# New order of steps in the late and the early pairs of an attention-and-MLP kernel, and weights put together 1024 columns at a time

## The chip, the cores and the metric

The kernel runs on one core of a Trainium2 chip. The metric is the device time of one execution in microseconds (us). Engines are named as in the profile: PE (matrix products), PEld (its weight loads), DVE (vector engine), ACT (scalar engine), POOL (GpSimd), SP (the queue that issues the DMA transfers).

## The reference

Block-causal attention over 8 batches, 8 heads, 576 positions and 64 dimensions, and then a gated MLP on the 4608 rows of 512 that come out:

```
scores = scale * q @ k.T                    # masked by blocks of 64
attn   = exp(scores - max) / (sum + 1e-9)
x      = attn @ v                           # -> (4608, 512)
a = x @ w1 ; b = x @ w2                     # (512, 1024) each
out = ((a * b) @ w3) @ w_out                # (1024, 1024), (1024, 512)
```

The four weights are 64-bit floats; q, k and v are 32-bit.

## The kernel before, in words

The work is cut into 32 *pairs* (8 batches times 4 pairs of heads; one head is half j = 0 of the pair, the other j = 1). For each half the scores are computed in five tiles in PSUM, exponentiated by ACT, and multiplied with V. In the late pairs each 32-bit operand is split into a high and a low part, so that three products of a faster format give 32-bit accuracy.

**Early pairs 0 to 3** run while the weights arrive. `gen_w` loads the weights as pairs of 32-bit words, and `load_w` (L135) makes 32-bit floats of them on ACT (L150) and DVE (L151, L152, L155). `load_split` (L159) and `load_rows` (L164) then split w1 and w2 into high and low parts. The product w3 @ w_out is formed on PE (L388) and split (L376, L377). One call of the generator handles 512 columns of 128 rows, 512 KB of DMA.

**Late pairs 4 to 31** mix attention with the MLP: `gen_moe` works on blocks of 512 rows. For each of 8 blocks *f* of the hidden size it runs 8 steps of three matmuls (L412), then DVE multiplies both sides (L418), ACT makes the high part (L419) and POOL the low part (L420). Then come 4 x 8 steps of the second product (L430). After the last pair, the rest of the MLP runs alone.

The order of a pair is a string of letters, one for each half: `PLAN` (L44) for the late pairs, `EARLY_PLAN` (L49) for the early ones. The letters:

- S: one of the five score tiles (L243), then ACT's exponentials (L258, L259), DVE's subtract for the low part (L261) and POOL's running row sum (L264)
- V: one of five steps of the product with V (L306, early L282); V5 is the last and reads the 64-column low part that L261 wrote last
- F: one step of three matmuls of the MLP
- M: one step of `shift_mask` for the next pair: first ACT's casts (L171), then six groups of matmuls (L192) each followed by DVE's row maxima (L196); at the eighth step L198, a transpose on PE (*mt*, L200), ACT's negation (L202) and a DMA (L209) that writes the shift into qk
- A, B: `prep_qk` for the next pair's half 0 and for the pair's own half 1: a cast (L171, DVE), then a DMA that copies the high part (L219) and a subtract (L220, POOL in the late pairs); B also sends the other half of the shift and, at its second step, starts the load of the next pair's q and k (L100)
- R: DVE's sum over the row sums (*part*, L319); N: takes the result out of PSUM (L337, L338); T: a matmul of the sums (*tot*, L323), the reciprocal, and the division (L325 to L350)
- Q: brings in V for the next pair; C: one call of `gen_w`

The score tiles and the mask groups have two PSUM buffers each, so every second one waits for its reader; *tot* and *mt* use the same two buffers as the mask groups.

In the late pairs PE runs exactly in the written order. All other engines, and PE in the early pairs, are ordered ahead of time by a planner that takes what is ready by its own estimates, with the written order as priority; the early attention has a higher priority than the weights. The first six F are left out (`DELAY`), so that each late pair begins at the third step of an f block.

Of the kernel before, what the change touches and what calls it, by code (L numbers as in the profile page):

```python
# [7 lines left out]
F32 = mybir.dt.float32  # L8
# [4 lines left out]
ALU = mybir.AluOpType  # L13
# [3 lines left out]
P = 128  # L17
B, H, S, D = 8, 8, 576, 64
# [4 lines left out]
DF = 1024  # L23
NT = B * S
NC = DM // P
NF = DF // P
# [5 lines left out]
BIG = 8.0e9  # L32

PC = [0, 576, 1024, 1344, 1536]
PW = 1600
QLO = [0, 128, 256, 384, 512]
# [1 line left out]
PE = [0, 448, 768, 960, 1024]  # L40

PLAN = (  # L44
    "B F B S S F F B S S F F F F S M F F V V F V V F F R V F Q N F",
    "M A S F S F A S M F M S F M S F M A M V V V F F V V N Q R T M F F F",
)

EARLY_PLAN = (  # L49
    "M S S S C S C C C C M S V V B C M M V A V M V M Q B M A B M N",  # L50
    "S C C S A S S C S C V V V V V Q N T",
)

DELAY = 6
# [5 lines left out]
def block_causal_attention__then__gated_mlp_kernel(ctx, tc, qkv, consts, ident_in, w1, w2, w3t, wout, out_t):  # L60
    nc = tc.nc
    w1, w2, w3t, wout = (w.bitcast(I32) for w in (w1, w2, w3t, wout))
# [13 lines left out]
    w1l = cpool.tile([P, NC, DF], F32R, name="w1l")  # L76
    wh = cpool.tile([P, NF, DM], F32R, name="wh")
    wl = cpool.tile([P, NF, DM], F32R, name="wl")

    qk = [cpool.tile([P, 4, S], F32R, name=f"qk{j}") for j in range(2)]
# [7 lines left out]
    tl = {}  # L91
# [40 lines left out]
        tl["gh"] = pool.tile([P, NF, TB], F32R, name="gh")  # L132
        tl["gl"] = pool.tile([P, NF, TB], F32R, name="gl")

    def load_w(dst, src, k):  # L135

        t = tl["early"].tile([P, 1024], F32, tag="wraw", name="wraw", bufs=5)
        u = tl["early"].tile([P, 512], F32, tag="wbits", name="wbits", bufs=6)
        wide = t.bitcast(I32)
        nc.sync.dma_start(out=wide.rearrange("p (k w) -> p k w", k=k), in_=src)
        wide = wide.rearrange("p (c two) -> p c two", two=2)
        low, high = wide[:, :, 0], wide[:, :, 1]
        bits = u.bitcast(I32)
        V = nc.vector
        nc.scalar.activation(u, high.bitcast(F32), AF.Abs, scale=2.0**-112)  # L150
        V.tensor_scalar(out=bits, in0=bits, scalar1=3, scalar2=0x7FFFFFF8, op0=ALU.logical_shift_left, op1=ALU.bitwise_and)  # L151
        V.scalar_tensor_tensor(out=bits, in0=high, scalar=-0x80000000, in1=bits, op0=ALU.bitwise_and, op1=ALU.bitwise_or)  # L152
        if dst is None:
            dst = u.unsqueeze(1)
        V.scalar_tensor_tensor(out=dst.bitcast(I32), in0=low.rearrange("p (k w) -> p k w", k=k), scalar=29,  # L155
                               in1=bits.rearrange("p (k w) -> p k w", k=k), op0=ALU.logical_shift_right, op1=ALU.bitwise_or)
        return u

    def load_split(dst_h, dst_l, src):  # L159
        val = load_w(None, src.unsqueeze(1), 1)  # L160
        nc.scalar.copy(dst_h, val)
        nc.vector.tensor_tensor(out=dst_l, in0=val, in1=dst_h, op=ALU.subtract)

    def load_rows(dst_h, dst_l, src, c):  # L164
        for h in range(2):
            cs = slice(h * 512, (h + 1) * 512)
            load_split(dst_h[:, c, cs], dst_l[:, c, cs], src[c * P : (c + 1) * P, h * 1024 : (h + 1) * 1024])
            yield

    def cast(n, dst, src, act):  # L170
        (nc.scalar.copy if 0 < n <= EARLY or act else nc.vector.tensor_copy)(dst, src)  # L171
# [193 lines left out]

    def gen_w(wp):
        wo = tl["wo"]
        for k in range(NF):
            load_w(wo[:, k : k + 1, :], wout[k * P : (k + 1) * P, :].unsqueeze(1), 1)
            yield  # L370
        rows1 = (None for c in range(NC) for _ in load_rows(w1h, w1l, w1, c))
        pending = []

        def evacuate():
            m, acc = pending.pop(0)
            nc.scalar.copy(wh[:, m, :], acc)  # L376
            nc.vector.tensor_tensor(out=wl[:, m, :], in0=acc, in1=wh[:, m, :], op=ALU.subtract)  # L377

        for m in range(NF):
            t3 = wp.tile([P, NF, P], F32, tag="w3", name="w3", bufs=2)  # L380
            for k in range(0, NF, 4):
                src = w3t[k * P : (k + 4) * P, 2 * m * P : 2 * (m + 1) * P].rearrange("(k p) f -> p k f", p=P)
                load_w(t3[:, k : k + 4, :], src, 4)
                if k == 0:
                    yield
            acc = ps_m.tile([P, 512], F32, tag="psm", name=f"w{m}")
            for k in range(NF):
                nc.tensor.matmul(acc, t3[:, k, :], wo[:, k, :], start=(k == 0), stop=(k == NF - 1))  # L388
            pending.append((m, acc))
            if len(pending) > 1:  # L390
                evacuate()
            yield
            next(rows1)
            yield
        while pending:
            evacuate()
        for c in range(NC):
            yield from load_rows(w2h, w2l, w2, c)

    def gen_moe(k):  # L400
        mp, xh, xl, gh, gl = tl["late"], tl["xh"], tl["xl"], tl["gh"], tl["gl"]
        sides = ((w1h, w1l), (w2h, w2l))
        for f in range(NF):
            fs = slice(f * P, (f + 1) * P)
            acc = [ps_m.tile([P, TB], F32, tag="psm", name="ab") for _ in sides]
            order = [(i, c) for i in range(2) for c in range(NC)]
            if f == 0:
                order.sort(key=lambda ic: (ic[1] == NC - 1, ic))
            for i, c in order:
                a, b2 = sides[i]  # L410
                for s, (l, r) in enumerate(((a, xh), (b2, xh), (a, xl))):
                    nc.tensor.matmul(acc[i], l[:, c, fs], r[c], start=(c == 0 and s == 0), stop=(c == NC - 1 and s == 2))  # L412
                if (i, c) == (0, NC - 1):
                    a32 = mp.tile([P, TB], F32, tag="a32", name="a32", bufs=2)
                    nc.scalar.copy(a32, acc[0])
                if (i, c) != order[-1]:
                    yield
            nc.vector.tensor_tensor(out=a32, in0=acc[1], in1=a32, op=ALU.mult)  # L418
            nc.scalar.copy(gh[:, f, :], a32)  # L419
            nc.gpsimd.tensor_tensor(out=gl[:, f, :], in0=a32, in1=gh[:, f, :], op=ALU.subtract)  # L420
            if f == NF - 1:
                st["free"] = k + 1
                split_ready()
            yield
        for e in range(DM // P):
            t = ps_m.tile([P, TB], F32, tag="psm", name="o")
            es = slice(e * P, (e + 1) * P)
            for f in range(NF):
                for s, (l, r) in enumerate(((wh, gh), (wl, gh), (wh, gl))):
                    nc.tensor.matmul(t, l[:, f, es], r[:, f, :], start=(f == 0 and s == 0), stop=(f == NF - 1 and s == 2))  # L430
                if f < NF - 1:
                    yield
            o32 = mp.tile([P, TB], F32, tag="o32", name="o32")
            nc.scalar.copy(o32, t)
            nc.sync.dma_start(out=out_t[es, k * TB : (k + 1) * TB], in_=o32)
            yield
# [16 lines left out]
    def pair(n):  # L453
# [9 lines left out]
        for j in range(2):  # L463
# [2 lines left out]
            tiles = iter(S_TILES)  # L466
            pvs = (pv_early if early else pv)(n, j, xps, p_early)
            delay = DELAY if n == NPAIR and j == 0 else 0
            for step in (EARLY_PLAN if early else PLAN)[j].split():
                if step == "C":  # L470
                    fill(weights, 1)
                    continue
# [101 lines left out]
```

## Time and profile before

| | |
|---|---|
| runs shown | 1099.05, 1101.97, 1103.21 us; median 1101.97 |
| profiled execution | 1099.04 us, span 1097.3 us |
| PE busy | 988.5 us (90%) |
| DVE busy | 777.6 us (71%) |
| ACT busy | 535.6 us (49%) |
| POOL busy | 527.3 us (48%) |
| mean granted clock of PE | 0.966 |
| moved by DMA | 80.12 MB |

Busy shares are means over stages with different limits, and a matmul's end is modelled, so a busy PE is not PE at its peak. What matters is which engine waits for which, stage by stage.

### The profile page before, as it was taken

What the parts mean: (1) busy time and instruction counts of PE and PEld (TensorE: products, weight loads), DVE (VectorE), ACT (ScalarE), POOL (GpSimd) and SP (SyncE); (2) the same over time, 40 slices, a digit from 0 to 9 for tenths busy, and PEclk for the clock granted to TensorE, in tenths of its full rate; (3) what the DMA queues carried; (4) which work ended last, traced back from release to release, by engine and by line L of the source; (5) the groups of instructions that cost most, each with busy time, mean ns of one, the idle gap of its engine ahead of it and who ended that gap; (6) DMA issues with size and microseconds to landing.
All of it is one profiled execution on the core that took longest, in us unless ns stands there. A gap on an engine that the chain in (4) does not pass through costs nothing.

```text
span 1097.3 us, 13914 instructions
## 1 busy us (share of the span) xinstructions
PE 988.5 (90%) x4608; PEld 763.6 (70%) x4608; DVE 777.6 (71%) x1284; ACT 535.6 (49%) x1265; POOL 527.3 (48%) x449
## 2 busy tenths in 40 slices
PE   4799978989988898899999898899889988999998
PEld 2454557777777777777777677677777777888887
DVE  7899987877888678877887777777877887611010
ACT  4565655555455554545555544545554455422121
POOL 0000075665567455755666555754675567423020
PEclk9899989999999999999999999999999999999999
DMA  7867311222222222222112222221222211000001
GB/s 242 257 222 247 90 49 52 56 75 75 56 57 62 68 65 56 56 63 75 36 54 64 75 56 56 65 85 45 56 56 84 66 45 33 30 10 10 29 1 39
DMA packets 37112, 80.12 MB, mean 73 GB/s; under 512 B 4464, under 2 KB 12784, under 8 KB 37040
## 3 DMA queue, kind: packets, MB, share of 16 engines
q1 hardware_dynamic: 37040, 79.23, 24.6%
q8 instruction: 36, 0.59, 0.2%
q14 instruction: 36, 0.29, 0.1%
HBM read 50.76 MB, written 9.44 MB: 55 GB/s over the span
## 4 chain that ended last, share of the span: by engine, by line
PE 60%; DVE 28%; ACT 6%; issue 5%; DMA 1%; SPq 0%; ACTq 0%; DVEq 0%
PE ab L412 28%; PE o L430 16%; DVE m L196 7%; DVE ph L261 6%; PE s L243 6%; DVE pl L261 5%; PE x L306 4%; PE w L388 3%; DVE qk L171 2%; ACT rsum L258 2%; DVE part L319 2%; ACT ph L259 1%; PE tot L323 1%; DVE qk L220 1%; DVE wbits L152 1%
## 5 line engine op out<-in xcount | busy, mean ns | idle before, releaser
L264 POOL TENSOR_TENSOR rsum<-rsum,p 128x448 f32<-128x448 f32 x224 | 184.4, 823 | 113.8 <-ACT p L258 86.7
L420 POOL TENSOR_TENSOR gl<-a,gh 128x512 fp32r<-128x512 f32 x72 | 98.1, 1362 | 196.4 <-ACT gh L419 196.4
L243 PE MATMUL s<-qk 128*128 128x288 f32 (+4 forms) x768 | 164.1, 320 | 17.4 <-ACT ph L259 5.3
L261 DVE TENSOR_TENSOR pl<-p,ph 128x448 fp32r<-128x448 f32 x168 | 152.6, 922 | 37.7 <-ACT ph L259 36.1
L243 PEld LDWEIGHTS s<-qk 128*128 128x128 f32 (+1 forms) x768 | 123.4, 185 | 51.0 <-ACT ph L259 10.9
L220 POOL TENSOR_TENSOR qk<-rqk,qk 64x1152 fp32r<-64x1152 f32 x54 | 148.4, 2748 | 18.3 <-DVE qk L171 18.2
L233 POOL TENSOR_TENSOR vs<-rv,vs 128x320 fp32r<-128x320 f32 x56 | 49.2, 880 | 189.6 <-ACT vs L171 189.6
L196 DVE TENSOR_REDUCE m<-mx 128x1 f32<-128x512 f32 (+6 forms) x320 | 129.8, 446 | 5.0 <-PE mx L192 3.6
L259 ACT ACTIVATE ph<-s 128x288 fp32r<-128x288 f32 x336 | 131.4, 392 | 0.0
L412 PE MATMUL ab<-xh,w1h 128*128 128x512 f32 x288 | 126.1, 438 | 0.1
L418 DVE TENSOR_TENSOR a<-ab,a 128x512 f32<-128x512 f32 x72 | 49.2, 683 | 103.0 <-PE ab L412 102.3
L430 PE MATMUL o<-gh,wh 128*128 128x512 f32 x288 | 120.7, 419 | 0.0
L412 PE MATMUL ab<-xh,w2h 128*128 128x512 f32 x288 | 118.9, 413 | 0.0
L412 PE MATMUL ab<-xh,w1l 128*128 128x512 f32 x288 | 118.1, 410 | 0.0
L412 PE MATMUL ab<-xl,w1h 128*128 128x512 f32 x288 | 118.0, 410 | 0.0
L430 PE MATMUL o<-gh,wl 128*128 128x512 f32 x288 | 116.6, 405 | 0.0
L430 PE MATMUL o<-gl,wh 128*128 128x512 f32 x288 | 116.2, 403 | 0.0
L412 PE MATMUL ab<-xl,w2h 128*128 128x512 f32 x288 | 114.7, 398 | 0.0
L258 ACT ACTIVATE p<-s 128x448 f32<-128x448 f32 x224 | 86.1, 384 | 58.2 <-PE s L243 41.4
L412 PE MATMUL ab<-xh,w2l 128*128 128x512 f32 x288 | 114.1, 396 | 0.0
L306 PE MATMUL x<-ph,vs 128*128 128x128 f32 x336 | 89.7, 308 | 13.6 <-DVE ph L261 13.6
L192 PE MATMUL mx<-kb,qd 128*128 128x512 bf16 (+6 forms) x320 | 73.6, 297 | 25.4 <-DVE m L196 18.1
(69 smaller groups left out, 1796.6 us busy)
## 6 DMA issues: line engine op xcount, KB each, us to landing
qk<-qk SPq DMA_DIRECT2D x64, 288.0 KB
rqk<-in_qkv SPq DMA_DIRECT2D x31, 576.0 KB
rv<-in_qkv SPq DMA_DIRECT2D x32, 320.0 KB
out_t<-o SPq DMA_DIRECT2D x36, 256.0 KB
wraw<-in_w3t SPq DMA_DIRECT2D x16, 512.0 KB
wraw<-in_w SPq DMA_DIRECT2D x16, 512.0 KB
wraw<-in_wout SPq DMA_DIRECT2D x8, 512.0 KB
qk<-ms SPq DMA_DIRECT2D x64, 2.2 KB
```

What stands on the lines that cost most here:

```text
L192: nc.tensor.matmul(sc, qd[:, i, :], kb[:, a:b], start=True, stop=True)
L196: nc.vector.reduce_max(m[:, col : col + 1], sc, axis=AX.X)
L220: (nc.vector if n <= EARLY else nc.gpsimd).tensor_tensor(out=low, in0=rqk[o], in1=high, op=ALU.subtract)
L243: nc.tensor.matmul(t[ks, at : at + q1 - q0], qk[j][:, 2 + s, kr], qk[j][:, s, q0:q1], start=(s == 0), stop=(s == 1))
L258: nc.scalar.activation(p32, t[ks, at : at + w], AF.Exp, scale=SCALE)
L259: nc.scalar.activation(ph[ks, o : o + w], t[ks, at : at + w], AF.Exp, scale=SCALE)
L261: nc.vector.tensor_tensor(out=low, in0=p32, in1=ph[ks, o : o + w], op=ALU.subtract)
L264: nc.gpsimd.tensor_tensor(out=r, in0=r, in1=p32, op=ALU.add)
L306: nc.tensor.matmul(xps[:, to : to + w], v[:, c, :], parts[s][:, a : a + w], start=(u < 2 and s == 0), stop=((u, s) in ((0, 1), (len(PV) - ...
L412: nc.tensor.matmul(acc[i], l[:, c, fs], r[c], start=(c == 0 and s == 0), stop=(c == NC - 1 and s == 2))
L420: nc.gpsimd.tensor_tensor(out=gl[:, f, :], in0=a32, in1=gh[:, f, :], op=ALU.subtract)
L430: nc.tensor.matmul(t, l[:, f, es], r[:, f, :], start=(f == 0 and s == 0), stop=(f == NF - 1 and s == 2))
```

## The change

Three things are edited. The late pair's two strings are new; both orders hold 24 F, 10 S and 10 V. The early pairs get a pair of strings each instead of one common pair; C stands 20 times in all instead of 40. And `load_w` takes a width: w_out and w3 come in loads of 1024 columns (1 MB), as do the rows of w1 (one row block whole) and of w2 (two row blocks, half the columns each). The buffers of a load go from five of 1024 words to three of 2048, those of the bits from six of 512 to two of 1024. `load_split` is folded into `load_rows`. An assertion at build time was added, which issues nothing.

```diff
 PLAN = (
-    "B F B S S F F B S S F F F F S M F F V V F V V F F R V F Q N F",
-    "M A S F S F A S M F M S F M S F M A M V V V F F V V N Q R T M F F F",
+    "F F F F F S F S F B S F F B S F M F S F F V V V V V Q M R N F",
+    "S S M F S F F S M F V S M R M F F V F F V V M F V N Q F T A A M",
 )
 EARLY_PLAN = (
-    "M S S S C S C C C C M S V V B C M M V A V M V M Q B M A B M N",
-    "S C C S A S S C S C V V V V V Q N T",
+    ("S S S V S S C V C B M C M M A V V V M N M B M M Q M",
+     "S S C S A V C S S V V V V Q N T C"),
+    ("C M S S V S M C V C S V B C S A V V M M Q B M N A M",
+     "S M S M C S V V S V S V V N T Q"),
+    ("M B M S S S B V C S V S V V V Q N M",
+     "S S V M A S M V S A C M C S M V V M V N T Q"),
+    ("S C B C S V S C S S B V M V A M M V M V N Q",
+     "C S S M S S V V S V A V V Q C N M T M C M"),
 )
...
-    def load_w(dst, src, k):
-        t = tl["early"].tile([P, 1024], F32, tag="wraw", name="wraw", bufs=5)
-        u = tl["early"].tile([P, 512], F32, tag="wbits", name="wbits", bufs=6)
+    def load_w(dst, src, k, n=1024):
+        t = tl["early"].tile([P, 2 * n], F32, tag="wraw", name="wraw", bufs=3)
+        u = tl["early"].tile([P, n], F32, tag="wbits", name="wbits", bufs=2)
...
+    def load_rows(dst_h, dst_l, src, c, k, cs):
+        rows = src[c * P : (c + k) * P, 2 * cs.start : 2 * cs.stop].rearrange("(k p) f -> p k f", p=P)
+        val = load_w(None, rows, k, k * (cs.stop - cs.start))
+        nc.scalar.copy(dst_h[:, c : c + k, cs], val)
+        nc.vector.tensor_tensor(out=dst_l[:, c : c + k, cs], in0=val, in1=dst_h[:, c : c + k, cs], op=ALU.subtract)
...
-        for k in range(NF):
-            load_w(wo[:, k : k + 1, :], wout[k * P : (k + 1) * P, :].unsqueeze(1), 1)
+        for k in range(0, NF, 2):
+            load_w(wo[:, k : k + 2, :], wout[k * P : (k + 2) * P, :].rearrange("(k p) f -> p k f", p=P), 2)
             yield
...
-            for k in range(0, NF, 4):
-                src = w3t[k * P : (k + 4) * P, 2 * m * P : 2 * (m + 1) * P].rearrange("(k p) f -> p k f", p=P)
-                load_w(t3[:, k : k + 4, :], src, 4)
-                if k == 0:
-                    yield
+            load_w(t3, w3t[:, 2 * m * P : 2 * (m + 1) * P].rearrange("(k p) f -> p k f", p=P), NF)
...
-            next(rows1)
-            yield
+            if m % 2:
+                load_rows(w1h, w1l, w1, m // 2, 1, slice(0, DF))
+                yield
...
-        for c in range(NC):
-            yield from load_rows(w2h, w2l, w2, c)
+        for h in range(2):
+            for c in (0, 2):
+                load_rows(w2h, w2l, w2, c, 2, slice(h * 512, (h + 1) * 512))
+                yield
...
-            for step in (EARLY_PLAN if early else PLAN)[j].split():
+            for step in (EARLY_PLAN[n] if early else PLAN)[j].split():
```

More of the change, by code (lines that the diff above doesn't have):

```diff
@@ L44 @@
 PLAN = (
-    "B F B S S F F B S S F F F F S M F F V V F V V F F R V F Q N F",
-    "M A S F S F A S M F M S F M S F M A M V V V F F V V N Q R T M F F F",
+    "F F F F F S F S F B S F F B S F M F S F F V V V V V Q M R N F",
+    "S S M F S F F S M F V S M R M F F V F F V V M F V N Q F T A A M",
 )
 EARLY_PLAN = (
-    "M S S S C S C C C C M S V V B C M M V A V M V M Q B M A B M N",
-    "S C C S A S S C S C V V V V V Q N T",
+    (
+        "S S S V S S C V C B M C M M A V V V M N M B M M Q M",
+        "S S C S A V C S S V V V V Q N T C",
+    ),
+    (
+        "C M S S V S M C V C S V B C S A V V M M Q B M N A M",
+        "S M S M C S V V S V S V V N T Q",
+    ),
+    (
+        "M B M S S S B V C S V S V V V Q N M",
+        "S S V M A S M V S A C M C S M V V M V N T Q",
+    ),
+    (
+        "S C B C S V S C S S B V M V A M M V M V N Q",
+        "C S S M S S V V S V A V V Q C N M T M C M",
+    ),
 )
@@ L152, in load_w @@
         V.scalar_tensor_tensor(out=bits, in0=high, scalar=-0x80000000, in1=bits, op0=ALU.bitwise_and, op1=ALU.bitwise_or)
+        val = u.rearrange("p (k w) -> p k w", k=k)
         if dst is None:
-            dst = u.unsqueeze(1)
+            dst = val
         V.scalar_tensor_tensor(out=dst.bitcast(I32), in0=low.rearrange("p (k w) -> p k w", k=k), scalar=29,
                                in1=bits.rearrange("p (k w) -> p k w", k=k), op0=ALU.logical_shift_right, op1=ALU.bitwise_or)
[L157 to L167, printed above, removed]
-            yield
+        return val
+    def load_rows(dst_h, dst_l, src, c, k, cs):
[3 more added lines that the diff above has]
+        nc.vector.tensor_tensor(out=dst_l[:, c : c + k, cs], in0=val, in1=dst_h[:, c : c + k, cs], op=ALU.subtract)
     def cast(n, dst, src, act):
@@ L367, in gen_w @@
         wo = tl["wo"]
-        for k in range(NF):
-            load_w(wo[:, k : k + 1, :], wout[k * P : (k + 1) * P, :].unsqueeze(1), 1)
+        for k in range(0, NF, 2):
+            load_w(wo[:, k : k + 2, :], wout[k * P : (k + 2) * P, :].rearrange("(k p) f -> p k f", p=P), 2)
             yield
-        rows1 = (None for c in range(NC) for _ in load_rows(w1h, w1l, w1, c))
         pending = []
@@ L392, in gen_w @@
             yield
-            next(rows1)
-            yield
+            if m % 2:
+                load_rows(w1h, w1l, w1, m // 2, 1, slice(0, DF))
+                yield
         while pending:
             evacuate()
-        for c in range(NC):
-            yield from load_rows(w2h, w2l, w2, c)
+        for h in range(2):
+            for c in (0, 2):
+                load_rows(w2h, w2l, w2, c, 2, slice(h * 512, (h + 1) * 512))
+                yield
     def gen_moe(k):
@@ L409, in gen_moe @@
             for i, c in order:
+                assert (k, c) in st["split"]
                 a, b2 = sides[i]
```

## The prediction, made before the changed kernel was run

> **What bounds the kernel now.** I began with the stages: the engines' busy time by stretches of the span, cut where the early pairs end (140 us), at the first score matmul of pair 5 and of pair 31, and at the end.
>
> ```profile
> 0.00:140.00 140.00, 113.84 (x379) 60.94 (x379) 125.88 (x242) 82.39 (x157) 1.87 (x7) 0.96 0.66 208
> 140.00:172.30 32.30, 25.68 (x112) 20.28 (x113) 28.58 (x41) 19.02 (x46) 24.56 (x20) 0.82 0.26 74
> 172.30:935.30 763.00, 690.68 (x3408) 551.91 (x3407) 595.89 (x963) 395.13 (x987) 464.11 (x392) 0.97 0.21 59
> 935.30:1097.30 162.00, 158.31 (x712) 130.49 (x710) 27.25 (x41) 39.08 (x77) 36.79 (x31) 1.00 0.05 20
> ```
>
> Columns: stretch, length, busy us of PE, PEld, DVE, ACT and POOL, granted clock, DMA share, GB/s. The early stage is DVE's (125.88 of 140.00). The last stage is nearly pure PE, and the change leaves it alone. The third row holds 26 late pairs: 763.00 / 26 = 29.35 us each, PE busy 690.68 / 26 = 26.56. So PE stands still 2.78 us a pair; and a clock of 0.97 costs 0.03 x 763 / 26 = 0.88 us more. These 3.66 us are all that a new order of the late pair can win: 27 pairs with such a tail x 3.66 = 99 us. DVE's 595.89 / 26 = 22.9 us lies below the remaining 25.7.
>
> Next I read PE's waits over the span (total, times, longest):
>
> ```profile
> PE tot L323 <- DVE m L198: 44.2, 27, 1.6
> PE mx L192 <- DVE m L196: 18.1, 32, 0.7
> PE x L306 <- DVE ph L261: 13.6, 27, 0.5
> ```
>
> Together 75.9 us, or about 2.8 a pair: the whole idle time is three waits, once a pair. The timeline of PE in pair 12 shows where:
>
> ```profile
> 389.95 0.61 PE L243 MATMUL s<-qk 128*128 128x288 f32 x2
> ...
> 396.18 0.39 PE L192 MATMUL mx<-kb,qd 128*128 128x320 bf16 x2
> 397.16 0.30 PE L192 MATMUL mx<-kb,qd 128*128 128x256 bf16 x2 [0.59 <-DVE m L196]
> ...
> 398.56 0.40 PE L412 MATMUL ab<-xh,w2h 128*128 128x512 f32 x1
> ...
> 399.26 0.40 PE L412 MATMUL ab<-xh,w2h 128*128 128x512 f32 x1
> ...
> 400.95 0.30 PE L306 MATMUL x<-ph,vs 128*128 128x64 f32 x1 [0.49 <-DVE ph L261]
> 402.88 0.41 PE L323 MATMUL tot<-part,ident 128*128 128x36 f32 x2 [1.64 <-DVE m L198]
> 403.13 0.28 PE L200 MATMUL mt<-ident,m 128*9 128x128 f32 x1
> ...
> 406.01 0.69 PE L243 MATMUL s<-qk 128*128 128x288 f32 x4
> ```
>
> From the second half's first S (389.95) to mt (403.13), PE waits three times in the last 7 us. The rows 398.56 and 399.26 give the length of an F step: 0.70 us. DVE in the same stretch, and the one POOL row that matters:
>
> ```profile
> 397.14 0.76 DVE L171 CAST qk<-rqk 64x1152 fp32r<-64x1152 f32 x1
> ...
> 398.32 2.57 DVE L261 TENSOR_TENSOR ph<-p,ph 64x64 fp32r<-64x64 f32 x1
> 400.93 1.22 DVE L196 TENSOR_REDUCE m<-mx 128x1 f32<-128x320 f32 x4
> 402.06 0.77 DVE L319 TRANSPOSE_TENSOR_REDUCE part<-rsum 128x18 f32<-128x576 f32 x1
> 402.75 0.11 DVE L198 TENSOR_REDUCE m<-m 128x1 f32<-128x2 f32 x1
> ```
>
> ```profile
> 397.98 2.83 POOL L220 TENSOR_TENSOR qk<-rqk,qk 64x1152 fp32r<-64x1152 f32 x1 [0.70 <-DVE qk L171]
> ```
>
> DVE is busy without a break. Its 64-column subtract takes 2.57 us and ends as POOL's L220 ends (400.81); over the kernel the same form takes:
>
> ```profile
> L261 DVE TENSOR_TENSOR ph<-p,ph x56: 225/510/2579, 151.8 to 954.4; 64x64 fp32r<-64x64 f32 x56
> ```
>
> (ns, least/median/most.) So 2.57 - 0.23 = 2.3 us of it is waiting for POOL. Also: the cast at 397.14 belongs to step B of the next pair. The planner moves the other engines' work far ahead of its step; only PE's order is the written one. That is why I cost the change by PE's order.
>
> The clock, by stretches:
>
> ```profile
> 396.20:403.20 7.00, 4.28 (x26) 3.46 (x25) 6.54 (x12) 1.43 (x5) 4.51 (x4) 1.00 0.39 95
> 432.10:435.50 3.40, 3.40 (x10) 2.66 (x9) 3.26 (x7) 2.50 (x5) 0.48 (x1) 0.50 0.40 129
> ```
>
> A tail has 7.00 - 4.28 = 2.7 us without PE work, and behind the next pair's tail PE runs 3.40 us at half clock.
>
> **The late pair, part by part.** Both orders hold 24 F, 10 S and 10 V; one B and one A fewer are calls that did nothing, and M is 8 in both. So no work goes: it is a new order.
>
> *Second half, tot and mt.* Old, from the first S to mt: 6 F, and PE needs 403.13 - 389.95 = 13.2 us less its three waits, 10.5. New: 9 F, and 10.5 + 3 x 0.70 = 12.6. DVE took 402.86 - 389.95 = 12.9 us for what stands in front of mt. In the new order one maximum (0.6) falls before the first S, and the product that ends an f block, a 512-wide instruction of about 0.7, comes ahead of the last maxima: 13.0. It is short by 0.4 if the 2.3 us behind POOL stay, by nothing if they go. But POOL's instructions fall into a shorter pair:
>
> ```profile
> L261 DVE TENSOR_TENSOR pl<-p,ph 128x448 fp32r<-128x448 f32 x168 | 152.6, 922 | 37.7 <-ACT ph L259 36.1
> ...
> L261 DVE TENSOR_TENSOR ph<-p,ph 64x64 fp32r<-64x64 f32 x56 | 80.4, 1435 | 1.9 <-ACT ph L259 0.2
> ...
> L261 DVE TENSOR_TENSOR pl<-rsum,ph 128x288 fp32r<-128x288 f32 x112 | 68.8, 625 | 38.9 <-ACT ph L259 37.0
> ```
>
> The subtracts, which wait for POOL, take 301.8 / 56 = 5.4 us a half; POOL's share goes from 464.11 / 763.00 = 0.61 to 17.9 / 27.2 = 0.66, 8% more, 0.4 us. I take 0.4 + 0.4 = 0.8. The ends: nothing, and 1.6 if the cast of A (0.76), so far in the first half, also falls ahead of mt. R now stands ahead of the last two maxima, so part is early and tot's 1.64 is gone; what is late next is mt, behind L198.
>
> *The last maxima group.* Old: two groups back to back (396.18, 397.16), wait 0.59. Now four F and three V stand between them, but the two groups before are adjacent (S M R M): the second needs DVE's maxima of two groups earlier, about 2 us before it. Between 0 and 0.59, I take 0.3.
>
> *V5.* Last S to V5: three F old, five F and two more groups new, some 1 us more. The wait of 0.49 goes; should the block stay, it comes out of the same lateness of DVE that I count at mt.
>
> *First half.* V5 stands nearer to the last S: F F V V V V, 2 x 0.70 + 1.5 = 2.9 us. The rows of pair 13:
>
> ```profile
> 411.60 0.45 PE L243 MATMUL s<-qk 128*128 128x192 f32 x4
> ```
>
> ```profile
> 413.29 0.32 ACT L258 ACTIVATE p<-s 128x192 f32<-128x192 f32 x1
> ```
>
> ```profile
> 414.99 0.51 DVE L261 TENSOR_TENSOR ph<-p,ph 64x64 fp32r<-64x64 f32 x1
> ```
>
> ```profile
> 414.71 1.11 POOL L264 TENSOR_TENSOR rsum<-rsum,p 128x192 f32<-128x192 f32 x2
> 415.78 2.67 POOL L220 TENSOR_TENSOR qk<-rqk,qk 64x1152 fp32r<-64x1152 f32 x1
> ```
>
> The subtract ended at 415.50, 3.45 us after the last S (412.05), but ACT began 1.1 us late there, behind an f block's end; the new order ends blocks at the 6th and the 14th F, away from this place. 3.45 - 1.1 = 2.35 < 2.9: no wait. If L220 took its 2.67 us ahead of the subtract, 2.35 + 2.3 - 2.9 = 1.8. POOL's adds stand before L220 here, so I take 0.2.
>
> *A, B and the last M with their DMAs.* A's copy on SP and POOL's L220 are done as soon as the score tiles free qk, whatever the step's place, as 397.14 shows. The last M still sends the shift by SP:
>
> ```profile
> 400.84 0.34 SPq L100 DMA_DIRECT2D rqk<-in_qkv  x1
> 403.73 0.80 SPq L209 DMA_DIRECT2D qk<-ms  x1
> ```
>
> Old: mt 403.13, next S 406.01, no wait, 2.88 us. New: five F, 3.5 us. Cost nothing; but SP is one queue, and the load of rqk (behind B's L220) stands ahead of the shift by 2.9 us: were L220 later than that, the next S would wait, up to its 2.8 us.
>
> *Sum.* Waits: 0.8 + 0.3 + 0.2 = 1.3 left of 2.78, 1.48 won. The half clock follows a tail with 2.7 us idle in 7; waits under 1 us and apart should seldom bring it: of 0.88 I leave 0.25 (between 0 and 0.88), 0.63 won. 27 x (1.48 + 0.63) = 57 us.
>
> The Trainium skill ("TensorE: Matmul & The Clock Gate", Part 1, What's actually happening) says that the clock halves after at least one idle window of about 3.4 us. By that rule no wait left here could halve it and the sum would be 27 x 0.25 = 7 us better; but this trace shows the half clock where no single wait exceeds 1.64 us, so the rows decide.
>
> **The early pairs.** The costliest groups of DVE in the first 140 us, and a late one for the slope:
>
> ```profile
> L152 DVE SCALAR_TENSOR_TENSOR wbits<-wraw,wbits 128x512 int32<-128x512 int32 x40 | 27.0, 683 | 0.3
> ...
> L151 DVE TENSOR_SCALAR wbits<-wbits 128x512 int32<-128x512 int32 x40 | 16.3, 417 | 0.8 <-ACT wbits L150 0.7
> L220 DVE TENSOR_TENSOR qk<-rqk,qk 64x1152 fp32r<-64x1152 f32 x10 | 13.4, 1343 | 1.0 <-ACT qk L171 0.8
> ```
>
> ```profile
> L338 DVE TENSOR_TENSOR x<-x,xlow 64x576 f32<-64x576 f32 x56 | 42.3, 755 | 75.1 <-ACT xlow L337 74.2
> ```
>
> 576 more columns cost 1343 - 755 = 588 ns, so 512 more about 0.52: one of 1024 takes 1.21 us where two took 1.37. There are 40 x 3 bit instructions and 16 splits, 136, which become 68: 68 x 0.15 = 10 us of DVE at most. Against it, the buffers go from five and six to three and two, so fewer loads interleave, and the last block of 1024 ends with a longer chain of its own before the late stage may begin. DMA bytes are the same, in 20 loads for 40. Ends: 10 us gained, or 8 lost if two such blocks (about 4 us of DVE each) fall behind the last early pair. I take 5 gained.
>
> **The sum.** 1099.04 (the profiled execution; its span 1097.3) - 57 - 5 = 1037. The median of the runs shown, 1101.97, stands 2.9 above that execution, so 1040.
>
> **Rivals.**
> *DVE stays late* and the wait only moves from tot to mt: 1.6 + 0.59 + 0.1 = 2.3 us of waits stay and 0.73 of the clock's. Won: 0.63 x 27 + 5 = 22: 1080. For it: DVE has no gap in the tail, and the same instructions remain. Against it: 3 more F ahead of tot.
> *All of it goes*: 99 + 10: 993. For it: 25.7 us leave DVE 2.8 us of room. Against it: POOL's 464.11 / 26 = 17.9 us a pair fall into a shorter time and delay DVE oftener.
> *Slower, by one mechanism: POOL's L220 goes ahead of the 64-column subtract in both halves.* Then 1.6 + 0.59 + 1.8 = 4.0 us of waits, the half clock in proportion 1.27: 5.27 against 3.66, 27 x 1.6 = +43, less 5: 1140. It decides when the waits pass 2.9 a pair, which is L220 ahead in some 40% of the first halves besides all the second ones. For it: the 2.57 row, and a V5 that is closer; against it: 414.71 before 415.78. The Trainium skill ("SBUF — State Buffer", SBUF: two separate sides) calls the port that VectorE and GpSimd share an exclusive lock held for the whole instruction; the 2.57 us agree.
> *The early order does nothing* (the planner arranges it as before): 5 us less won, inside the forecast's range.
>
> **Chances.** Forecast 0.56 (its own range 1018 to 1062); wait moves 0.20 (1062 to 1093); nearly all gone 0.14 (985 to 1018); within 0.5% (5.5 us, about what this kernel's runs can tell) 0.03; slower 0.07. So faster 0.90, and 8 in 10 lie within 998 to 1088.
>
> **What would show it.** A pair of 27.2 us instead of 29.35 between first S tiles; no wait of tot, and mt or the mask group with under 1 us; the granted clock at 0.99 from 172 us on; the subtract in the first half near 0.5 us and V5 unhindered; the first late S at about 130 instead of 135 to 138 us. I am wrong if PE waits at V5 of the first half for ph, if S waits for the shift's DMA, or if DVE's waits behind POOL grow with the shorter pair.

## The result, and the profile after

The changed kernel takes 991.55 us (median of four runs, 990.67 to 991.80) against 1101.61 for the kernel before: a ratio of 0.900, interval 0.898 to 0.902. The prediction was 1040, with 1018 to 1062 as its own range and 998 to 1088 for eight cases in ten; the measured time lies below both. The gain is 110 us where 62 were forecast. The time is that of the rival *all of it goes*, 993 us. The profiled execution took 990.67 us, its span 988.9.

The stages of the kernel after, cut at the first S of pairs 4, 5 and 31 (columns as in the prediction's first view):

```profile
0.00:130.00 130.00, 109.92 (x375) 58.63 (x375) 118.72 (x170) 78.42 (x127) 1.87 (x7) 1.00 0.67 222
130.00:161.40 31.40, 26.86 (x130) 21.66 (x130) 27.32 (x45) 18.95 (x46) 23.82 (x20) 0.89 0.28 79
161.40:829.40 668.00, 652.78 (x3407) 544.10 (x3406) 543.72 (x964) 395.68 (x990) 479.54 (x392) 1.00 0.25 68
829.40:988.90 159.50, 155.67 (x700) 128.30 (x698) 25.80 (x39) 38.34 (x76) 34.65 (x31) 1.00 0.05 20
```

A late pair takes 668.00 / 26 = 25.69 us instead of 29.35. Idle time of PE fell from 2.78 to (668.00 - 652.78) / 26 = 0.59 us, the granted clock is 1.00, and PE's busy time fell by (690.68 - 652.78) / 26 = 1.46 us a pair. The span shrank by 95.0 us here, by 10.9 ahead of pair 5 (172.3 to 161.4) and by 2.5 in the last stage. DVE's busy time fell too, from 22.9 to 20.9 us a pair, while the share of POOL rose from 0.61 to 479.54 / 668.00 = 0.72.

PE's largest waits of the late pairs (us in all, times, longest):

```profile
PE mx L192 <- DVE m L196: 7.7, 17, 0.8
PE s L243 <- ACT ph L259: 5.4, 12, 1.2
...
PE ab L411 <- ACT a L414: 3.5, 10, 0.5
```

Together 16.6 us instead of 75.9; the waits of *tot* and of V5 are gone. The 64-column subtract, over the kernel (ns: least/median/most; before 225/510/2579):

```profile
L261 DVE TENSOR_TENSOR ph<-p,ph x56: 227/231/235, 144.3 to 845.7; 64x64 fp32r<-64x64 f32 x56
```

It never waits for POOL any more. The timelines of POOL, DVE and PE in one second half show why:

```profile
483.50 3.92 POOL L264 TENSOR_TENSOR rsum<-rsum,p 128x448 f32<-128x448 f32 x4 [0.49 <-ACT p L258]
487.49 2.67 POOL L220 TENSOR_TENSOR qk<-rqk,qk 64x1152 fp32r<-64x1152 f32 x1
```

```profile
485.39 1.17 DVE L171 CAST qk<-rqk 64x1152 fp32r<-64x1152 f32 x1
486.60 0.65 DVE L261 TENSOR_TENSOR pl<-p,ph 128x192 fp32r<-128x192 f32 x1
487.27 0.23 DVE L261 TENSOR_TENSOR ph<-p,ph 64x64 fp32r<-64x64 f32 x1
...
490.70 0.16 DVE L198 TENSOR_REDUCE m<-m 128x1 f32<-128x2 f32 x1
```

```profile
485.41 0.38 PE L192 MATMUL mx<-kb,qd 128*128 128x320 bf16 x2 [0.45 <-DVE m L196]
...
491.06 0.31 PE L323 MATMUL tot<-part,ident 128*128 128x36 f32 x2
491.20 0.28 PE L200 MATMUL mt<-ident,m 128*9 128x128 f32 x1
```

L220 has two conditions: the cast, and POOL's own adds ahead of it. Before, the cast came last: L220 waited 0.70 us for it and then started 0.34 us ahead of the 64-column subtract. Now the cast is over at 486.56, POOL's four adds at 487.42, and L220 begins as the subtract (487.27 to 487.50) ends. DVE reaches the end of L198 at 490.86, ahead of PE's mt.

### The profile page after: what moved, and what is told of

It reads as the page before. It is cut to its first block, busy times and chain, and to the rows that moved or that the text cites. A ratio compares the mean times of both kernels' runs of the same rounds, so it can differ in the third digit from the quotient of the medians.

```text
span 988.9 us, 13818 instructions
## 1 busy us (share of the span) xinstructions
PE 945.2 (96%) x4608; PEld 752.7 (76%) x4608; DVE 715.6 (72%) x1216; ACT 531.4 (54%) x1237; POOL 539.9 (55%) x449
## 4 chain that ended last, share of the span: by engine, by line
PE 56%; POOL 11%; DVE 11%; ACT 9%; DMA 8%; issue 5%; POOLq 0%; ACTq 0%; SPq 0%; DVEq 0%
PE ab L411 25%; PE o L429 14%; DMA rqk<-in_qkv 8%; PE s L243 7%; POOL rsum L264 6%; PE x L306 6%; POOL qk L220 5%; ACT qd L171 2%; DVE m L196 2%; PE mx L192 2%; PE w L383 2%; DVE pl L261 2%; DVE wbits L156 1%; ACT kb L171 1%; PE x L282 1%
## 5 line engine op out<-in xcount | busy, mean ns | idle before, releaser
L264 POOL TENSOR_TENSOR rsum<-rsum,p 128x448 f32<-128x448 f32 x224 | 201.1, 898 | 67.7 <-ACT p L258 41.5
L419 POOL TENSOR_TENSOR gl<-a,gh 128x512 fp32r<-128x512 f32 x72 | 93.5, 1299 | 172.3 <-ACT gh L418 172.3
L261 DVE TENSOR_TENSOR pl<-p,ph 128x448 fp32r<-128x448 f32 x168 | 145.9, 874 | 33.1 <-ACT ph L259 32.1
L243 PE MATMUL s<-qk 128*128 128x288 f32 (+4 forms) x768 | 157.8, 306 | 11.3 <-ACT ph L259 5.4
L220 POOL TENSOR_TENSOR qk<-rqk,qk 64x1152 fp32r<-64x1152 f32 x54 | 144.1, 2668 | 2.0
L233 POOL TENSOR_TENSOR vs<-rv,vs 128x320 fp32r<-128x320 f32 x56 | 57.0, 1018 | 141.7 <-ACT vs L171 141.7
L411 PE MATMUL ab<-xl,w1h 128*128 128x512 f32 x288 | 113.6, 395 | 1.1 <-POOL xl L364 1.1
L411 PE MATMUL ab<-xh,w1l 128*128 128x512 f32 x288 | 113.3, 393 | 0.0
L261 DVE TENSOR_TENSOR pl<-rsum,ph 128x288 fp32r<-128x288 f32 x112 | 81.8, 731 | 33.5 <-ACT ph L259 30.0
L418 ACT CAST gh<-a 128x512 fp32r<-128x512 f32 x72 | 44.7, 621 | 113.0 <-DVE a L417 112.7
```

Source lines behind the costliest of these rows:

```text
L220: (nc.vector if n <= EARLY else nc.gpsimd).tensor_tensor(out=low, in0=rqk[o], in1=high, op=ALU.subtract)
L233: nc.gpsimd.tensor_tensor(out=v[:, :, oth[j]], in0=rv, in1=v[:, :, own[j]], op=ALU.subtract)
L243: nc.tensor.matmul(t[ks, at : at + q1 - q0], qk[j][:, 2 + s, kr], qk[j][:, s, q0:q1], start=(s == 0), stop=(s == 1))
L261: nc.vector.tensor_tensor(out=low, in0=p32, in1=ph[ks, o : o + w], op=ALU.subtract)
L264: nc.gpsimd.tensor_tensor(out=r, in0=r, in1=p32, op=ALU.add)
```

## Experiments

Each ratio is against the kernel before, run beside it (1100.6 to 1103.4 us), with its 95% interval.

### What belongs to which part

**Late strings alone** (kernel before with the new `PLAN`):

> The kernel before with the late pair's two strings alone (early pairs and weight loads as before). From the two traces: pairs 5 to 30 took 763 us before and 668 after, pair 4 some 6 us less, the part after pair 31's first S 2.5 us less. Theory 1 (all of this is the late order's): 1101.6 - 95 - 6 - 2.5 = 998 us. Theory 2 (pair 4's 6 us come from the weights being ready sooner): 1004 us. If the early edits did more than move the start, 1010 or more.

999.07 us, ratio 0.9066 [0.9052, 0.9079]: 102.6 us of the 110.

**Early order and 1024 columns alone** (kernel after with the old `PLAN`):

> The changed kernel with the late pair's old strings: the early orders and the 1024-column weights alone. Theory 1: the first S of pair 4 comes 4.9 us sooner and nothing else changes, 1096.7 us. Theory 2: pair 4 gains too, 1091 us.

1094.31 us, 0.9933 [0.9913, 0.9952]: 7.4 us. The two parts add up to 110.0.

**Width without the early order** (four of the ten C of a pair are taken out of the old strings, the other letters stay; the 20 calls of `gen_w` are thus through after the second C of the fourth pair):

```diff
-    "M S S S C S C C C C M S V V B C M M V A V M V M Q B M A B M N",
-    "S C C S A S S C S C V V V V V Q N T",
+    ("M S S S C S C C M S V V B C M M V A V M V M Q B M A B M N",
+     "S C S A S S C S V V V V V Q N T"),
+) * 4
```

> Old late strings; the 1024-column weights with the old early string, of which every second C is left out (20 calls instead of 40). If the fewer and longer DVE instructions are what the early part gains (68 x 0.07 to 0.15 us), 1092 to 1097 us. If the new early orders are what counts, 1101 us or, with coarser pieces in the wrong place, slower.

1102.82 us, 1.0006 [0.9994, 1.0018]: nothing.

**Early order without the width** (the kernel before; the new early strings, each C written twice):

> Old late strings and 512-column weights; the new early orders with each C doubled (40 calls). The other side of the width run: if width is what gains, 1101 us here; if order is, 1095 to 1097 us.

1099.31 us, 0.9979 [0.9970, 0.9989]: 2.4 us. Three rows with the first and the last start: with the width alone, DVE's splits of w2 and ACT's late exponentials; with the order alone, DVE's splits of w2:

```profile
L156 DVE TENSOR_TENSOR w2l<-wbits,w2h x4: 1183/1218/1226, 100.0 to 122.2; 128x1024 fp32r<-128x1024 f32 x4
```

```profile
L246 ACT ACTIVATE p<-s x224: 205/385/606, 147.2 to 957.2; 128x448 f32<-128x448 f32 x56, 128x192 f32<-128x192 f32 x56
```

```profile
L176 DVE TENSOR_TENSOR w2l<-wbits,w2h x8: 676/688/694, 107.4 to 139.6; 128x512 fp32r<-128x512 f32 x8
```

With the width alone the weights are done at 123 us, but the attention of pair 4 comes no earlier (first late exponential at 147.2, in the kernel before at 144.9). With the order alone the weights last to 140, as before. In the kernel after they are done at 132 and the exponential comes at 138.3. So the late stage seems to need both, and each alone is worth little of the 7.4 us.

### The two halves of the late pair

The kernel after with one late string at a time put back. **Old first half** (one M added behind Q, so that eight remain):

```diff
-    "F F F F F S F S F B S F F B S F M F S F F V V V V V Q M R N F",
+    "B F B S S F F B S S F F F F S M F F V V F V V F F R V F Q M N F",
```

> The kernel after, with the first half of a late pair in the order of before (one M added, behind Q, so that the eight stay). Theory now: the first half counts, because POOL's L220 of step B starts the load of the next q and k, ACT's in-order queue stands behind that load with its casts, and the new half has five F and a spread of S while this goes on. Then a wait of the first half's S for ACT's ph comes back, about 1 us a pair, some 30 to 40 us in all: 1020 to 1030 us. Rival, which is the prediction's own view (the first half's order costs nothing): 990 to 996 us, a pair stays at 25.7 us and the wait of S for ACT below 10 us in all.

**Old second half** (without its first M):

```diff
-    "S S M F S F F S M F V S M R M F F V F F V V M F V N Q F T A A M",
+    "A S F S F A S M F M S F M S F M A M V V V F F V V N Q R T M F F F",
```

> The kernel after, with the second half of a late pair in the order of before (without its first M, which the new first half has). Theory now: the second half holds most of the gain. The 64-column subtract of L261 takes about 2.58 us again behind POOL's L220, the waits of tot, of the last mask group and of the fifth V come back with some 70 us in all, and half clock with them: a pair of 28.5 to 29.4 us, 1065 to 1095 us. Rival: if the first half was what took POOL's L220 away from the subtract, the subtract stays near 0.23 us and only the lack of cover ahead of tot counts, 20 to 30 us: 1010 to 1025 us.

1069.49 us (0.9700 [0.9682, 0.9718]) and 1094.54 us (0.9929 [0.9910, 0.9949]); the second lies where the theory put it, the first 40 us above. With both old halves it is 1094.31, with both new ones 991.55. So the new first half alone is worth nothing, the new second half alone 25 us, and both together 103: most of the gain is an interaction. PE's waits with the old first half, its mt and the next S of one pair, and PE's waits with the old second half:

```profile
PE s L243 <- DMA qk<-ms: 58.9, 28, 3.4
```

```profile
503.45 0.28 PE L200 MATMUL mt<-ident,m 128*9 128x128 f32 x1
504.26 0.29 PE L243 MATMUL s<-qk 128*128 128x288 f32 x1
506.89 0.67 PE L243 MATMUL s<-qk 128*128 128x288 f32 x3 [2.33 <-DMA qk<-ms]
```

```profile
PE tot L323 <- DVE m L198: 42.9, 27, 1.6
PE mx L192 <- DVE m L196: 25.9, 55, 1.5
PE x L306 <- DVE ph L261: 13.1, 26, 0.5
```

The new second half moves three F from behind mt to ahead of *tot*. These three F had covered the shift's way from mt over SP into qk. The five F at the start of the new first half cover it instead; without them S waits 2.1 us a pair for the shift. With the old second half the three old waits are all back.

**Five F in front, score tiles as close as before:**

```diff
-    "F F F F F S F S F B S F F B S F M F S F F V V V V V Q M R N F",
+    "F F F F F B B S S F F B S S F F S M F F V V F V V F R V Q M N F",
```

> The kernel after, with the first half's five leading F kept, and behind them the score tiles as close together as before (two B, then S S F F B S S F F S). It separates two things that the old first half changed at once. If only the five leading F counted (they cover the shift's DMA, which cost 58.9 us of waits with the old first half), the wait of S for the shift stays away and the time is 990 to 1000 us. If the spread of the score tiles counts too, because ACT's exponentials stand in its queue behind the casts that wait for the load of q and k, S waits for ACT's ph by 1 us a pair or more: 1015 to 1035 us.

1017.03 us, 0.9221 [0.9196, 0.9247]: in the band of the second theory, but not by its mechanism. S waits 7.4 us for ACT in all, hardly more than the 5.4 of the kernel after. What came is the wait of V5:

```profile
PE x L306 <- DVE ph L261: 13.6, 12, 1.2
```

```profile
464.03 2.76 POOL L220 TENSOR_TENSOR qk<-rqk,qk 64x1152 fp32r<-64x1152 f32 x1
```

```profile
464.31 2.56 DVE L261 TENSOR_TENSOR ph<-p,ph 64x64 fp32r<-64x64 f32 x1
```

In a first half, L220 goes 0.28 us ahead of the subtract. That is the prediction's mechanism for *slower*, in 12 of the 28 first halves. So the spread of the score tiles does count: it keeps POOL's L220 behind the subtract in the first half too. Of the 25.5 us, 16.5 are waits of the product with V for L261 (13.6, and 2.9 for its other parts); where the other 9 lie I could not settle.

### POOL ahead of the subtract

**Short L220 in the kernel before**: the second half's L220 works on 64 of its 1152 columns.

```diff
+        if n > EARLY and j == 1:
+            nc.gpsimd.tensor_tensor(out=low[:, :, 0:32], in0=rqk[o][:, :, 0:32], in1=high[:, :, 0:32], op=ALU.subtract)
+        else:
...
```

> The kernel before, with POOL's subtract L220 of the late pairs' second half cut to 64 of its 1152 columns (the rest of that low part is left out), so that it can't hold up DVE's 64-column subtract. Port theory (DVE is late because it stands 2.3 us behind L220, and PE's own 10.5 us would else nearly do): the subtract takes 0.23 us, the waits at V5 and tot go, 2.1 us a pair, and most of the half clock, 0.6: 1101.6 - 27 x 2.7 = 1029 us. Cover theory (DVE has too much work there anyway, only F steps ahead of tot help): under 27 x 0.7 gained, 1083 us or more.

1037.47 us, 0.9410 [0.9396, 0.9424]: 65 us without any new order. The waits of *tot* and V5 are gone; a new one stands in their place:

```profile
PE s L246 <- ACT ph L262: 22.3, 27, 4.8
```

A short L220 also takes POOL time away (400.48 us in 26 pairs for 464.11), and what stands behind it on POOL and SP starts sooner, so the 65 us are not the block's alone.

**Two POOL adds less in the kernel after**: in the second half two of the four row-sum adds are left out, so that POOL reaches L220 earlier.

```diff
-            if c > 0:
+            if c > 0 and not (j == 1 and c >= 3):
```

> The changed kernel without POOL's last two row-sum adds of the late pairs' second half (the row sums of three of nine blocks of keys are left out there), so that POOL is free for L220 before DVE's 192- and 64-column subtracts. It has less work. Port theory: L220 now holds them up by some 2 us, DVE ends L198 at 13.7 us against PE's 12.1: 1.6 us of waits a pair and part of the half clock, 991.5 + 27 x 2 = 1045 us. If the cover is ample or L220 doesn't block, 985 to 992 us.

1035.76 us, 0.9397 [0.9378, 0.9417]: with *less* work the kernel is 44 us slower than after. POOL, DVE and PE's waits:

```profile
509.06 2.75 POOL L220 TENSOR_TENSOR qk<-rqk,qk 64x1152 fp32r<-64x1152 f32 x1 [1.75 <-DVE qk L171]
```

```profile
507.35 0.78 DVE L319 TRANSPOSE_TENSOR_REDUCE part<-rsum 128x18 f32<-128x576 f32 x1 [0.62 <-POOL rsum L264]
...
509.34 2.55 DVE L261 TENSOR_TENSOR ph<-p,ph 64x64 fp32r<-64x64 f32 x1
```

```profile
PE mx L192 <- DVE m L196: 58.6, 44, 1.9
```

L220 waits for the cast again, starts 0.28 us ahead of the subtract, and holds it for its whole length; so it goes in 27 of the 28 second halves. DVE's order changed as well: the sum L319 now stands ahead of the cast and waits 0.62 us for POOL's row sums, so that the 44 us are the block's in the main (2.55 - 0.23 = 2.3 us a pair) and not alone. The order of these two instructions is an ingredient of the gain.

**L220 in two instructions, in the kernel before** (second half, one for q and one for k), and the same **without the loads of q and k from pair 6 on**:

```diff
+        if n > EARLY and j == 1:
+            for t in range(2):
+                nc.gpsimd.tensor_tensor(out=low[:, t], in0=rqk[o][:, t], in1=high[:, t], op=ALU.subtract)
+        else:
...
```

> The kernel before, with POOL's subtract L220 of the late pairs' second half written as two instructions of 576 columns; all work stays. Port theory: DVE's 64-column subtract gets in between the two, some 1.2 us sooner, PE's waits fall by as much and part of the half clock goes: 1101.6 - 27 x 1.6 = 1058 us. If it is POOL's load and not the length of the one instruction that delays DVE, 1095 to 1102 us.

> The kernel before, with POOL's L220 of the second half as two instructions (as in the run with the split alone), and in addition no loads of q and k from pair 6 on: the later pairs compute with the values of pair 5, and some 28 MB of DMA are left out. Theory now: with the split alone, S waits 32 us for ACT's ph because ACT's casts stand behind that load ahead of the exponentials. Without the load this goes, and the 13 us of S behind the shift's DMA in part: 1045 to 1060 us against 1092. Rival: ACT's casts do not matter, and S waits because POOL and DVE are late: 1085 to 1095 us.

The split: 1092.03 us, 0.9919 [0.9895, 0.9943], only 9 us. The subtract takes 1.35 us at most instead of 2.58, as it should if one POOL instruction is one hold, but a new wait eats the gain (subtract; PE; ACT):

```profile
L265 DVE TENSOR_TENSOR ph<-p,ph x56: 226/511/1346, 151.7 to 947.3; 64x64 fp32r<-64x64 f32 x56
```

```profile
PE s L247 <- ACT ph L263: 32.2, 26, 4.5
PE tot L327 <- DVE m L198: 31.0, 27, 1.2
...
PE s L247 <- DMA qk<-ms: 12.8, 10, 2.2
```

```profile
403.99 0.67 ACT L171 CAST kb<-rqk 128x576 bf16<-128x576 f32 x1 [2.40 <-DMA rqk<-in_qkv]
...
406.47 0.41 ACT L262 ACTIVATE rsum<-s 128x288 f32<-128x288 f32 x1
```

ACT works in the planned order. Its casts of the next pair's k and q stand ahead of the exponentials, and they wait for the load that B starts behind L220. Without the load it is 1039.51 us, 0.9436 [0.9418, 0.9453], 53 us less:

```profile
PE s L250 <- ACT ph L266: 4.9, 1, 4.9
```

S's wait for ACT is gone (32.2 to 4.9), as the queue theory has it; the time came out 6 us below its band. This wait and S's for the shift (12.8 to 3.5) make 37 of the 53 us; the other 16 are less busy time of PE (971.7 to 956.1 us), for which the runs show no cause. The run leaves out 15.4 MB of DMA (80.12 to 64.77), not 28.

**The kernel after without these loads:**

> The kernel after, with no loads of q and k from pair 6 on: the later pairs compute with the values of pair 5. Theory now: the new first half covers the load, so nearly nothing is won; PE's idle time is 0.59 us a pair, and of that only the 5.4 us of S behind ACT and the 3.5 us of ab behind ACT can go: 983 to 992 us. Rival: the load still sets the pace of the pairs in the new order (it stands in the chain of work that ended last): 975 us or less.

985.64 us, 0.8944 [0.8927, 0.8961]: 6 us less than after. So the load that costs the split variant 53 us is nearly covered in the new order, though it stands in the chain that ended last (7.5% of the span); its bytes alone are not what costs the 53 us.

### Cover

**Three F more ahead of *tot*, in the kernel before** (taken from behind mt; four F at the start of the first half), and **the same with six F at its start**:

```diff
-    "B F B S S F F B S S F F F F S M F F V V F V V F F R V F Q N F",
-    "M A S F S F A S M F M S F M S F M A M V V V F F V V N Q R T M F F F",
+    "B F F F F B S S F B S S F F S M F F V V F V V F F R V F Q N F",   (four)
+    "B F F F F F F B S S F B S S F S M F V V F V V F F R V F Q N F",   (six)
+    "M A S F S F A S M F M S F M S F M A M V V V F F V F F V N Q R F T M",
```

> The kernel before, with three F of the second half moved from behind the last M to ahead of V5 and tot, and three of the first half moved ahead of its first S, so that the shift is covered. L220 still goes ahead of the 64-column subtract. Cover theory: PE's own work from the first S to mt grows from 10.5 to 12.6 us against DVE's 12.9, the waits at V5 and tot shrink from 2.1 to 0.3 and the half clock goes: 1101.6 - 27 x 2.5 = 1034 us. Port theory: the late DVE only moves the wait, under 27 x 1 gained, 1075 us or more.

> As the run with three F moved ahead of V5 and tot, with two more F of the first half ahead of its first S, so that the shift's DMA is covered as well (S waited 25 us for it there). Cover theory: those 25 us come on top, 1081 - 25 = 1056 us. Port theory: DVE's lateness moves the wait on to the mask groups and the exponentials, 1068 us or more.

1081.34 us, 0.9808 [0.9792, 0.9825], and 1071.77 us, 0.9729 [0.9707, 0.9750]. PE's waits and the subtract in the first of them:

```profile
PE s L243 <- DMA qk<-ms: 25.4, 23, 2.2
...
PE tot L323 <- DVE m L198: 6.3, 27, 0.3
```

```profile
L261 DVE TENSOR_TENSOR ph<-p,ph x56: 230/2576/2595, 152.1 to 937.3; 64x64 fp32r<-64x64 f32 x56
```

The F take *tot*'s wait from 44.2 to 6.3 us, and S waits 25.4 us for the shift instead; six F in front take that down to 3.4. The block stays at 2.58 us, and in both runs it comes to 12 of the 28 first halves too (39 subtracts of over 2 us instead of 27), where the kernel before has none. So the 21 and 29 us are what this cover is worth with more blocks than before; cover with the blocks unchanged was not measured.

**The kernel after without the cover** (the three F behind mt again):

```diff
-    "S S M F S F F S M F V S M R M F F V F F V V M F V N Q F T A A M",
+    "S S M F S F F S M F V S M R M F F V F V V M V N Q T A A M F F F",
```

> The changed kernel with three F of the second half moved from ahead of V5 and tot to behind the last M; L220 still comes after the subtract. DVE needs 11.7 us from the first S to the end of L198 in the changed kernel, PE's own work is 10.0 there: cover theory: 1.7 us of waits a pair and half clock again, 991.5 + 27 x 2.2 = 1051 us. If the gone block alone explains the gain, 992 to 1000 us.

1061.50 us, 0.9626 [0.9607, 0.9645]: 70 us lost, though the subtract stays at 233 ns in the middle:

```profile
PE mt L200 <- DVE m L198: 43.4, 28, 1.6
...
PE tot L323 <- DVE m L196: 12.3, 27, 0.6
```

This is the rival *wait moves to mt*, and the granted clock is 0.97 again over the late pairs.

### Details that changed nothing, and one attempt

**R late, as before, in the kernel after** (R behind Q instead of between the mask groups):

> The changed kernel with R back behind Q, where it stood before. In the order for DVE only the sum and one pair of maxima change places, and the sum still ends 1.5 us before tot: 991.5 us, no change. If R's early place was part of the gain, as the prediction had it, tot waits up to 0.7 us a pair: up to 1010 us.

992.49 us, 0.9015 [0.8997, 0.9034]. The letter's place is worth nothing: the sum and a pair of maxima change places on DVE, and *tot* still does not wait.

**One F between the two adjacent mask groups** ("M R F M F V" for "M R M F F V"):

> The changed kernel with one F moved between the two adjacent mask groups of the second half (R F M F V for R M F F V). The longest wait left there is PE's for the maxima, 7.7 us in 17 times: if the F covers it, 984 to 987 us; if the same lateness shows at the next group or at V2, 991 us.

991.97 us, 0.9008 [0.8987, 0.9029]. The wait of mx falls from 7.7 to 1.1 us; those of S for ACT and of ab for ACT rise from 5.4 to 7.7 and from 3.5 to 5.6.

**Step B's L220 on DVE:**

```diff
-        (nc.vector if n <= EARLY else nc.gpsimd).tensor_tensor(out=low, in0=rqk[o], in1=high, op=ALU.subtract)
+        (nc.vector if n <= EARLY or j == 1 else nc.gpsimd).tensor_tensor(out=low, in0=rqk[o], in1=high, op=ALU.subtract)
```

> The kernel after, with step B's L220 (the low part of the second half) on DVE instead of POOL: an attempt at a faster kernel. It takes 1.34 us there instead of 2.67, so the load of the next q and k starts over 1.3 us sooner and POOL no longer takes part in that chain; DVE gets 1.34 us more in a pair of 25.7 of which it uses 20.9. If the load's chain is what the 0.59 us of idle time per pair is from: 983 to 989 us. Rival: those 1.34 us of DVE fall ahead of the last maxima and mt, and delay them by up to as much: waits of mx and mt rise by 10 to 30 us, 1000 to 1020 us.

1037.28 us, 0.9405 [0.9381, 0.9428], 46 us slower than after and beyond the rival's band. PE's waits:

```profile
PE mt L200 <- DVE m L198: 29.1, 22, 2.1
PE mx L192 <- DVE m L196: 19.3, 24, 1.4
```

The 1.35 us of DVE fall ahead of the last maxima, and the clock of the late pairs fell to 0.99. In 7 of the 28 second halves the 64-column subtract is held up besides: in one it starts at 318.56 and takes 2.72 us, while two POOL instructions of 1.3 us each (L364) run from 318.67 to 321.19. The runs do not separate the two. No variant that does the whole work was faster than the kernel after.

## Why the prediction was wrong, step by step

- **Right by luck: the bound.** 3.66 us a pair were said to be all that an order can win, and 29.35 - 25.69 = 3.66 were won, but they are not the same 3.66. Of the idle time 2.19 us went and 0.59 stayed; PE's busy time fell by 1.46, where the clock was to give 0.88 at most. The two differences cancel. Right as read are the three waits, the block behind POOL, DVE's place at the tail, and that no work goes.
- **Wrong: *Second half, tot and mt*, 0.8 us left a pair.** Nothing is left. 0.4 stood for the block's staying: it went from 2.57 to 0.23 us. The other 0.4 stood for subtracts growing with POOL's share: the share rose further than assumed, to 0.72 instead of 0.66, and the subtracts together took less. All L261 groups of the kernel after:

```profile
L261 DVE TENSOR_TENSOR pl<-p,ph 128x448 fp32r<-128x448 f32 x168 | 145.9, 874 | 33.1 <-ACT ph L259 32.1
...
L261 DVE TENSOR_TENSOR pl<-rsum,ph 128x288 fp32r<-128x288 f32 x112 | 81.8, 731 | 33.5 <-ACT ph L259 30.0
...
L261 DVE TENSOR_TENSOR ph<-p,ph 64x64 fp32r<-64x64 f32 x56 | 12.9, 231 | 1.7
```

  That is 240.6 / 56 = 4.3 us a half instead of 5.4. The 64-column form alone fell by 67.5 us (80.4 to 12.9); the others grew by 6.3 us in all, 0.1 a half where 0.4 was assumed. Which of the two instructions starts first mattered far more than how busy POOL is. The trace of before showed what decided it (L220 waiting 0.70 us for the cast), and I did not ask what the new order does to that. Two counts of this part are off and change nothing: from the first S to *mt* the orders hold 7 and 10 F, not 6 and 9 (three more, as the sum has it), and one more mask group stands between the last S and V5, not two.
- **Of the signs named:** the first late S is at 130.0 as foreseen, *tot*'s wait is gone, V5 is unhindered; the clock is 1.00 instead of 0.99, the pair is 25.69 instead of 27.2, and the subtract in the first half takes 0.23 instead of 0.5.
- **Right: *the last maxima group*.** 0.3 us a pair taken, 7.7 / 27 = 0.29 measured.
- **V5 and *first half*.** V5's wait went, and 0.2 us for the first half was 0 in the kernel after. The price behind it is real: the dense variant paid it, with L220 ahead of the subtract.
- **Right by its row, and more than it said: *A, B and the last M with their DMAs*.** "New: five F, 3.5 us. Cost nothing" holds. The old first half, which has one F ahead of its first S and closer score tiles, costs 78 us, and S waits 58.9 us for the shift there; with the five F kept and the tiles close it is 25.5 us. The prediction's sum had no term for what these F carry.
- **Mis-sized: the clock.** 0.25 us a pair was left, 0 measured; and the 26 pairs before have 15 windows of 3.41 us at half clock, 51.2 us, so an estimate of 25.6 / 26 = 0.98 for the whole instead of 0.88. PE's busy time fell by 1.46 a pair, 0.47 more than that, and the cause of this rest stays open. A full clock alone does not bring the fall: with three F more ahead of *tot* the clock is 1.00 too, and PE is busy for 682.50 us, 8 less than before.
- **Mis-sized: the early pairs.** 5 taken, 7.4 measured. One instruction of 1024 columns was put at 1.21 us and took 1.21 to 1.22; the groups of DVE's weight work fall by 9.2 us (10 at most was the estimate). The feared eight us behind the last early pair did not come; with the width alone the first late exponential did come later than before, by 2.3 us, and with the new early order as well it came 6.6 us sooner.

```profile
L156 DVE SCALAR_TENSOR_TENSOR wbits<-wraw,wbits 128x1024 int32<-128x1024 int32 x20 | 24.4, 1220 | 0.4
```

The failed step, then, is the sum's term *Second half, tot and mt*: it left 0.8 us a pair because it kept L220 ahead of the 64-column subtract at half weight and let the subtracts grow with POOL's share, when the new order puts L220 behind that subtract in every pair and leaves nothing. The 0.2 for the first half and the 0.25 for the clock were kept as if independent of it, and both came out at 0. In numbers: the sum won 2.11 us a pair, the kernel 3.65 (95.0 / 26). Of the 1.54 between them, 0.71 are idle time of PE (1.3 left in the sum, 0.59 measured, half of which is the mask group that the sum had right); 0.83 are busy time, 0.35 of it by the half clock and 0.47 open. *All goes*, at 0.14, came close in time, in part by the cancelling named above; its reason holds, since DVE had the room, and the argument put against it, that POOL would delay DVE oftener, did not come true.

## What to carry to other kernels

When two engines block each other, look for the condition that came last for the longer instruction and ask what the new order does to it; a share of busy time does not say who starts first. A reorder's gains do not add: the new second half was worth 25 us without the new first half, the first nothing without the second, and both 103. Where steps are moved as cover to one place, find what they covered at the old one and cover it again, here the shift's way through SP.

## What the runs showed of the hardware

In these traces the half clock comes in windows of 3.41 us, behind windows in which PE was busy for about half of the time or less. Twice two successive windows of the kernel before (third column: PE busy; third from the end: the granted clock):

```profile
428.72:432.13 3.41, 1.28 (x9) 0.92 (x9) 2.90 (x9) 1.18 (x3) 1.55 (x2) 1.00 0.56 164
432.13:435.54 3.41, 3.41 (x10) 2.67 (x9) 3.28 (x7) 2.51 (x5) 0.52 (x1) 0.50 0.40 127
...
783.71:787.12 3.41, 1.77 (x10) 1.47 (x10) 2.87 (x10) 1.56 (x4) 0.86 (x1) 1.00 0.54 173
787.12:790.53 3.41, 3.41 (x18) 2.86 (x18) 3.34 (x5) 3.36 (x8) 1.43 (x1) 1.00 0.35 97
```

Behind 1.28 of 3.41 us busy (0.38) comes the half clock, behind 1.77 (0.52) it does not. The border lies near half and is not sharp: in the kernel before, the half clock also came behind one window of 1.73 and one of 1.77 (459.44 and 165.89), and in the variant with the old first half it did not come behind two of 0.49 and 0.50. One window there that ran at half clock itself, 0.71 busy, was followed by another at half clock. In these two kernels it is not the idle sum that counts but its clustering: 26 late pairs of the variant with three F more ahead of *tot* stand idle for 747.60 - 682.50 = 65 us, hardly less than the 72 of before, but spread out, and their clock is 1.00:

```profile
171.20:918.80 747.60, 682.50 (x3381) 527.66 (x3406) 603.43 (x965) 394.31 (x989) 469.65 (x393) 1.00 0.22 61
```

The Trainium skill ("TensorE: Matmul & The Clock Gate", Part 1, What's actually happening) gives the window of 3413 ns, and the rows agree; it says that an idle window halves the clock, and here a window that was 0.38 busy did.

A DVE subtract of 0.23 us took 2.55 to 2.57 us in the rows shown behind a POOL instruction of 2.75 to 2.83, and 1.35 at most behind one half as long. That is the lock for a whole instruction which the Trainium skill ("SBUF — State Buffer", SBUF: two separate sides) describes; what the runs add is its price in this kernel, most of 44 us where POOL has 0.28 us of a head start in each second half. The records do not say to the tenth of a microsecond who is first: with L220 on DVE, a subtract that starts 0.11 us ahead of POOL was held for the length of two POOL instructions.
